# RWKV-7 attention and dropless experts on one core: paired products share PSUM banks, and the PE order weighs array time against instruction count

## The chip, the core and the metric

The kernel runs on 1 core of one Trainium2 chip. The metric is the device time of one execution in microseconds (us), the median of several; lower is better. Engines are named as the profile names them: PE (TensorE's matmuls) and PEld (its weight loads), DVE (VectorE), ACT (ScalarE), POOL (GpSimd), SP (SyncE, which here only issues DMAs).

## The reference

Two parts run one after the other. The first is a recurrence over 768 time steps for 4 x 8 heads of width 40:

```python
for t in range(S):
    y[:, :, t] = einsum('bhd,bhde->bhe', r_t, state)
    Sa = einsum('bhde,bhe->bhd', state, a_t)
    state = state * w_t[:, :, None, :] - einsum('bhd,bhe->bhde', Sa, b_t)
    state = state + einsum('bhd,bhe->bhde', v_t, k_t)
```

Its output, 3072 rows of 320 numbers, goes into a mixture of 8 experts: each row takes the expert with the largest of 8 logits, `relu(x @ w1[e]) @ w2[e]`, times the softmax weight of that expert.

## The kernel before

**Attention.** Time is cut into 12 chunks of 64 steps, and the batch into two halves, which gives 24 units of work (`unit(u)`, line 395; u = 2 * chunk + half). Each unit holds 16 heads as eight blocks of 64x64 in tiles of 128 partitions. Within a chunk the recurrence becomes products of 64x64 blocks. A unit loads its operands by SP (`load`, line 411, four DMAs for each of dec, KB twice, A, V2, R, Vu), takes running products of the decays by two scans on DVE (rv and q, lines 432 and 440), scales KB and A by them on POOL (lines 447 and 449), and then works on PE in these products, each into PSUM and from there to SBUF by ACT or DVE:

- `p_ka` (line 458) and the two of `p_n` (473): KB with A, masked by DVE into Gk, T and N
- `p_sq` (497): N,T and T,N, copied into the first X; then three times `p_power` and `p_sum` (508, 534), which square X and carry a sum along; the copies go to ACT or DVE, the half-sums (lines 488 and 491, three instructions) to DVE. The last round gives M and TT, and `p_last` (557) makes TF of them. This is the X chain, which inverts a triangular matrix
- transposes of V2 and KB (lines 573, 583), `p_rhs` (605, with the state ST), a transpose of ST to Sn, `p_uT` (631), `p_yr` (647: the state's rows, Sn with R), `p_z` (655: Vu with R, masked into ZU), transposes of Vu, `p_y` (679: nKB with ZU, into the banks that `p_yr` began), which gives the output and the new state, and `p_x` (705), which turns the output for storage and makes the logits.

A 64x64 product uses one quarter of the array; most products take the four quarters in rotation (`TILES`), `p_ka` two of them. One matmul of the program stands in the trace as two matmuls and two weight loads (a transpose as one of each).

**What sets the order.** A unit only records steps. `in_order` (line 212) then plays them through with a cost in us for each: it takes at every point the step that can start first, of equals the one with the lowest rank (`key`, line 262), gives it PSUM banks from the 8 there are (`Held(n)` asks for n banks, from the first step that uses them to the last), and emits it on its engine's queue. Steps marked ANY go to ACT or DVE. A PE step's n is its count of instructions; the player lets PE take 256 of them (`PAGE`) per 3.6 us (`FETCH`). Buffers come in rings (`Ring`); a ring of 2 (dec) lets unit u + 2 load when unit u has been read. Engines take their queues strictly in order.

**Routing and experts.** Behind the attention the kernel sorts rows by expert (DVE, POOL and PE), then gathers them, and runs two dense layers per expert on PE. The weights of expert 0 are fetched into a pool of their own: `first_weights` (751) is a step of rank 8, those of the others follow when the attention's memory is free. The change touches none of this code but the place of that fetch and of the constants that the routing uses.

Of the kernel before, what the change touches and what calls it, by code (L numbers as in the profile page):

```python
# [23 lines left out]
def kernel(  # L24
# [62 lines left out]
    before = consts.tile([128, 128], F32)  # L87
    nc.gpsimd.memset(before[:], 1.0)
    nc.gpsimd.affine_select(
        before[:], before[:], compare_op=ALU.is_gt, fill=0.0, base=0, pattern=[[1, 128]], channel_multiplier=-1,  # L90
    )

# [22 lines left out]

    ones_sq = consts.tile([128, 128], F32)
    nc.gpsimd.memset(ones_sq[:], 1.0)
    zero_e = consts.tile([128, E], F32)
    nc.gpsimd.memset(zero_e[:], 0.0)
    keep = consts.tile([128, E, NT], F32)  # L120
    nc.gpsimd.memset(keep[:], 1.0)
    nc.gpsimd.memset(keep[:, :, 0:1], 0.0)

    def counted(name, shape, pattern, base, mult=0):
        ti = consts.tile(shape, I32, name=name + "_i")
        tf = consts.tile(shape, F32, name=name)
        nc.gpsimd.iota(ti[:], pattern=pattern, base=base, channel_multiplier=mult)
        nc.gpsimd.tensor_copy(tf[:], ti[:])
        return tf
# [9 lines left out]
    iota_r = consts.tile([128, 128], F16)  # L139
    nc.gpsimd.tensor_copy(iota_r[:], iota_f[:])  # L140
# [3 lines left out]
    nc.gpsimd.tensor_scalar(tokc[HP:], tokc[HP:], scalar1=float(S - C), scalar2=None, op0=ALU.add)  # L144
    tokv = consts.tile([128, NT], F32)
    nc.gpsimd.tensor_copy(tokv[:, :NCH], tokc[:])
    nc.gpsimd.tensor_scalar(tokv[:, NCH:], tokc[:], scalar1=-1.0, scalar2=None, op0=ALU.mult)
# [3 lines left out]
    nc.gpsimd.memset(turn_gate[:, :, 128:], 0.0)  # L151
    for par in range(2):
        nc.scalar.dma_start(
            turn_gate[par * HP : par * HP + D, :, 128:], moe_w_gate.rearrange("(p a e) n -> a e p n", a=2, e=D)[par],
        )
    nc.gpsimd.tensor_scalar(turn_gate[:, :, 128:], turn_gate[:, :, 128:], scalar1=-1.0, scalar2=None, op0=ALU.mult)
    nc.gpsimd.tensor_copy(turn_gate[:, :, :128], ident[:, None, :].to_broadcast([128, NP, 128]))
# [25 lines left out]
    PAGE, FETCH = 256, 3.6  # L183
# [28 lines left out]
    def in_order():  # L212
# [3 lines left out]
        page = [0, 0.0]  # L216
# [26 lines left out]
        while ready:  # L243
            times = sorted({f for f in bank_free if f is not None})
            best = None
            for s, r in ready.items():
                new = [h for h in s.ps if h.at is None]
                for e in ((ACT, DVE) if s.eng == ANY else (s.eng,)):
# [13 lines left out]
                    key = (t0, s.rank, t0 + cost)  # L262
# [38 lines left out]
    with tc.tile_pool(name="ring", bufs=1) as ring, \  # L301
# [23 lines left out]
        r_dec = Ring("dec", [SEG * C1 + 1], 2)  # L325
# [34 lines left out]
        for i in range(3):  # L360
            for j, r in enumerate((r_KB, r_A, r_V2, r_Vu, r_R)):
                if i < len(r.bufs):
                    t, held = r.bufs[i]
                    for lo in (32, 96):
                        zero(-99 + 9 * i + j, POOL if lo == 32 else DVE, 0.5, t[lo : lo + 32], held)
        for t, held in r_qini.bufs:
            zero(-98, POOL, 0.6, t[:], held)
        for r in (r_rhs, r_ST, r_S):
            for t, held in r.bufs:
                zero(-50, POOL, 0.6, t[:], held)  # L370
# [4 lines left out]
        def pair(h, width):  # L375
            return psum[:, h.at : h.at + 2, : NP * width].rearrange("x a (p d) -> x a p d", p=NP)
# [18 lines left out]
        def unit(u):  # L395
# [28 lines left out]
            other = ACT if u == 0 else SP  # L424
# [14 lines left out]
            Step(pre, DVE, 0.3, invert, reads=hrv, writes=hqi + hpc)  # L439
# [17 lines left out]

            def p_ka(e, ps=ps):
# [4 lines left out]
            Step(u, PE, 8 * ROUND, p_ka, reads=hKB + hA, writes=[ps], n=64)  # L463
            Step(u, DVE, 0.69, lambda e, ps=ps: nc.vector.tensor_tensor(
                Gk[:], psum[:, ps.at, :].rearrange("x (q p j) -> x q p j", p=NP, q=2),
                m_plus[:, None, None, :].to_broadcast([128, 2, NP, C]), op=ALU.mult,
            ), reads=[ps], writes=hGk)
            T1, hT1 = r_T.take()
            N1, hN1 = r_N.take()
            for t1, ht1, mask, turned_ in ((T1, hT1, m_up, False), (N1, hN1, m_low, True)):  # L470
                ps = Held(2)

                def p_n(e, ps=ps, turned_=turned_):
                    t = pair(ps, C)
                    for p in range(NP):
                        for par, z in TILES:
                            q = par ^ z
                            l, r = b_at(p, q, par), head(Aq, p, q, par)
                            mm(t[halves[z], q, p, :], *((r, l) if turned_ else (l, r)))
                Step(u, PE, 4 * ROUND, p_n, reads=hKB + hA, writes=[ps], n=64)  # L480
                Step(u, DVE, 0.69, lambda e, ps=ps, t1=t1, mask=mask: nc.vector.tensor_tensor(  # L481
                    t1[:], pair(ps, C), mask[:, None, None, :].to_broadcast([128, 2, NP, C]), op=ALU.mult,
                ), reads=[ps], writes=ht1)
# [10 lines left out]
            for i, (l, r) in enumerate(((T1, N1), (N1, T1))):  # L494
                ps = Held(2)

                def p_sq(e, ps=ps, l=l, r=r):
                    t = pair(ps, C)
                    for p in range(NP):
                        for h, s in TILES:  # L500
                            q = h ^ s
                            mm(t[halves[s], q, p, :], l[halves[h], q, p, :], r[halves[h], q, p, :])
                Step(u, PE, 4 * ROUND, p_sq, reads=hN1 + hT1, writes=[ps], n=64)
                Step(u, ANY, 0.59, lambda e, i=i, ps=ps, X=X: copy(e, X[:, :, :, i, :], pair(ps, C)), reads=[ps], writes=hX[i : i + 1])
            Step(u, DVE, 1.1, lambda e, X=X: sums(e, X[:, :, :, 2, :], ihalf[:, None, None, :].to_broadcast([128, 2, NP, C]), T1[:], False),
                 reads=hT1, writes=hX[2:3])

            def p_power(e, ps, X, l, r):
                t = pair(ps, C)
# [4 lines left out]

            k = 2
            while 4 * k <= C:

                end = 4 * k == C
                Xn, hXn = r_X.take() if not end else (None, None)
                ps = Held(2)  # L520
                Step(u, PE, 4 * ROUND, lambda e, ps=ps, X=X: p_power(e, ps, X, 1, 0), reads=hX[:2], writes=[ps], n=64)
                if end:
                    M, hM = r_M.take()
                    Step(u, DVE, 0.69, lambda e, ps=ps, M=M: nc.vector.tensor_tensor(M[:], pair(ps, C), eye(2, NP), op=ALU.add),  # L524
                         reads=[ps], writes=hM)
                else:
                    Step(u, ANY, 0.59, lambda e, ps=ps, Xn=Xn: copy(e, Xn[:, :, :, 0, :], pair(ps, C)), reads=[ps], writes=hXn[0:1])
                ps = Held(2)
                w = 1 if end else 2

                def half_sums(ps, w):
                    return psum[:, ps.at : ps.at + 2, : NP * w * C].rearrange("x b (p w j) -> x b p w j", p=NP, w=w)

                def p_sum(e, ps=ps, X=X, w=w):
# [487 lines left out]
```

## Time and profile before

| | before |
|---|---|
| median of 3 runs | 901.5 us (900.42 to 902.14) |
| the profiled execution: its own time | 899.75 us |
| its span in the trace, first to last instruction | 898.0 us |
| mean granted clock of TensorE | 0.955 |
| PE busy | 776.2 us (86%), 17128 matmuls |
| PEld busy | 606.5 us (68%), 17128 weight loads |
| DVE busy | 460.0 us (51%) |
| ACT busy | 234.5 us (26%) |
| POOL busy | 173.7 us (19%) |

Busy times are sums over the whole span; the stages have different limits, so a share of the span says little of any one of them. The granted clock is in shares of the full 2.4 GHz; it has two levels, 1.00 and 0.50.

### The profile page before, as it was taken

To read this page: it belongs to the slowest core of one execution; us is meant where nothing else is said; L and a number is where in the kernel's file an instruction comes from. 1 tells how busy PE (TensorE), PEld (TensorE's weight loads), DVE (VectorE), ACT (ScalarE), POOL (GpSimd) and SP (SyncE) were. 2 spreads that over 40 slices of the span, in tenths; PEclk is the share of its full clock that TensorE was granted. 3 is DMA by queue.
4 is the path that set the end of the run, shared out by engine and by line. 5 is a ranking of instruction groups with operands and counts; after the bars stand their busy time and mean duration, and the time that the engine had idled before them with its cause. 6 is when DMAs were issued, how large, how long until landed. Compare 5 with 4: busy or idle time off the path is not lost.

```text
span 898.0 us, 38059 instructions
## 1 busy us (share of the span) xinstructions
PE 776.2 (86%) x17128; PEld 606.5 (68%) x17128; DVE 460.0 (51%) x980; ACT 234.5 (26%) x502; POOL 173.7 (19%) x224
## 2 busy tenths in 40 slices
PE   0797789889998999899989998418999999999995
PEld 0686678788887888788878887416845545545543
DVE  6685578777676867687767676361110110120110
ACT  0343244333333334333433433100110110110110
POOL 9332111121202020202020100043211211001001
PEclk9999899999999989999999999656999999999998
DMA  5323313222322232223222200183313513402000
GB/s 165 89 67 86 86 45 69 65 65 60 71 67 61 57 71 64 56 61 75 62 57 60 48 12 12 22 259 96 95 53 107 187 60 114 132 14 83 10 13 23
DMA packets 136569, 65.16 MB, mean 73 GB/s; under 512 B 116881, under 2 KB 132243, under 8 KB 136404
## 3 DMA queue, kind: packets, MB, share of 16 engines
q1 hardware_dynamic: 130888, 52.76, 23.2%
q0 software_dynamic: 3136, 9.44, 3.4%
q8 instruction: 135, 2.21, 1.0%
q10 hardware_dynamic: 2380, 0.50, 0.3%
q14 instruction: 30, 0.25, 0.1%
HBM read 54.01 MB, written 9.31 MB: 71 GB/s over the span
## 4 chain that ended last, share of the span: by engine, by line
issue 36%; PE 30%; DVE 11%; DMA 9%; POOL 7%; SPq 3%; ACT 2%; POOLq 0%; ACTq 0%; DVEq 0%
PE ps L385 25%; DMA dec<-in_packed_dram 8%; PE ps L583 4%; DVE X L491 3%; POOL out_dram L917 3%; SPq L416 3%; POOL xg L875 2%; PE ps L573 2%; ACT X L380 2%; DVE X L488 1%; DVE q L440 1%; DVE T L481 1%; POOL KB L447 1%; DMA KB<-in_packed_dram 1%; DVE TT L491 0%
## 5 line engine op out<-in xcount | busy, mean ns | idle before, releaser
L385 PE MATMUL ps<-X 64*64 64x64 f32 (+1 forms) x6144 | 163.1, 243 | 22.2 <-DVE X L491 10.9
L385 PEld LDWEIGHTS ps<-X 64*64 64x64 f32 x6144 | 133.8, 135 | 42.2 <-DVE X L491 15.4
L901 DVE TENSOR_SCALAR h_sb<-hp 128x448 f32<-128x448 f32 (+2 forms) x44 | 21.8, 497 | 227.1 <-PE hp L900 225.8
L910 PE MATMUL zp<-w,h_sb 128*128 128x320 f32 (+1 forms) x512 | 123.8, 433 | 0.0
L380 ACT COPY X<-ps 128x512 f32<-128x512 f32 x152 | 88.3, 586 | 125.6 <-PE ps L385 119.9
L894 PE MATMUL hp<-xgT,w 128*128 128x448 f32 (+2 forms) x352 | 115.0, 473 | 3.7 <-DVE h_sb L901 2.3
L910 PEld LDWEIGHTS zp<-w,h_sb 128*128 128x128 f32 (+1 forms) x512 | 80.6, 177 | 37.5 <-issue 2.4
L894 PEld LDWEIGHTS hp<-xgT,w 128*128 128x128 f32 x352 | 60.9, 208 | 53.1 <-issue 48.9
L447 POOL TENSOR_TENSOR KB<-KB,rv 128x512 f32<-128x512 f32 x48 | 59.0, 1249 | 133.9 <-DMA A<-in_packed_dram 48.6
L449 POOL TENSOR_TENSOR A<-A,q 128x512 f32<-128x512 f32 x24 | 29.2, 1215 | 248.9 <-PE ps L385 83.8
L917 POOL DMA_INDIRECT out_dram<-zo,s_idx x28 | 27.6, 987 | 185.1 <-ACT zo L916 183.8
L491 DVE TENSOR_TENSOR X<-ps,X 64x256 f32<-64x256 f32 x144 | 60.8, 422 | 3.1
L902 ACT ACTIVATE h_sb<-hp 128x448 f32<-128x448 f32 (+2 forms) x44 | 19.3, 442 | 159.9 <-PE hp L900 121.6
L488 DVE TENSOR_TENSOR X<-ps,X 128x256 f32<-128x256 f32 x72 | 30.4, 422 | 46.4 <-ACT X L380 45.8
L385 PE MATMUL ps<-R,Vu 64*128 64x64 f32 x768 | 51.0, 284 | 2.5 <-issue 1.2
L385 PE MATMUL ps<-A,KB 64*64 64x64 f32 x1536 | 45.3, 224 | 9.0 <-DVE M L524 8.4
L385 PEld LDWEIGHTS ps<-R,Vu 64*128 64x128 f32 x768 | 47.4, 196 | 5.0 <-issue 2.4
L385 PEld LDWEIGHTS ps<-A,KB 64*64 64x64 f32 x1536 | 40.6, 138 | 12.0 <-DVE M L524 8.6
L432 DVE TENSOR_TENSOR_SCAN rv<-dec,ones 128x521 f32<-128x521 f32 x24 | 29.7, 1239 | 34.7 <-DMA dec<-in_packed_dram 22.8
L663 DVE TENSOR_TENSOR ZU<-ps,m_plus 128x512 f32<-128x512 f32 x48 | 30.9, 685 | 28.8 <-PE ps L385 28.6
L916 ACT COPY zo<-zp 128x320 f32<-128x320 f32 x28 | 11.9, 425 | 119.8 <-PE zp L910 115.9
L385 PE MATMUL ps<-ZU,nKB 128*64 128x104 f32 (+1 forms) x768 | 39.6, 257 | 1.0 <-DVE ZU L663 0.8
(178 smaller groups left out, 1066.1 us busy)
## 6 DMA issues: line engine op xcount, KB each, us to landing
w<-in_moe_w_dram SPq DMA_DIRECT2D x8, 1280.0 KB
w<-in_moe_w_dram SPq DMA_DIRECT2D x8, 1024.0 KB
KB<-in_packed_dram SPq DMA_DIRECT2D x188, 40.0 KB
x_rows<-xs SPq DMA_DIRECT2D x48, 96.0 KB
dec<-in_packed_dram SPq DMA_DIRECT2D x96, 40.0 KB
V<-in_packed_dram SPq DMA_DIRECT2D x96, 40.0 KB
Vu<-in_packed_dram SPq DMA_DIRECT2D x96, 40.0 KB
A<-in_packed_dram SPq DMA_DIRECT2D x92, 40.0 KB
```

Of the source, the lines that this page charges most:

```text
L380: nc.scalar.copy(dst, src)
L385: nc.tensor.matmul(out_, lhsT=lhsT, rhs=rhs, start=start, stop=stop, skip_group_check=True)
L432: Step(pre, DVE, 1.4, lambda e: nc.vector.tensor_tensor_scan(rv[:, : SEG * C1 + 1][:, ::-1], dec[:, ::-1], ones65[:, ::-1], 0.0, op0=ALU.m ...
L447: Step(pre, POOL, 1.25, lambda e, kb=kb, by=by: nc.gpsimd.tensor_tensor(kb, kb, by, op=ALU.mult), reads=hrv, writes=hKB[i : i + 1])
L449: Step(pre, POOL, 1.22, lambda e: nc.gpsimd.tensor_tensor(Aq[:], Aq[:], q3[:, :, :C], op=ALU.mult), reads=hq, writes=hA)
L488: nc.vector.tensor_tensor(dst[:, 0], src[:, 0], old[:, 0], op=ALU.add)
L491: nc.vector.tensor_tensor(dst[o_, 1], src[o_ if o else halves[h], 1], old[halves[h], 1], op=ALU.add)
L583: nc.tensor.transpose(psum[:, ps.at + b // NP, b % NP * 128 : (b % NP + 1) * 128], at(*divmod(b, 2)).rearrange("x s t -> x (s t)"), ident[:],)
L663: Step(u, DVE, 0.69, lambda e, s=s, ps=ps: nc.vector.tensor_tensor(ZU[:, s, :, :C], psum[:, ps.at + s, :].rearrange("x (b j) -> x b j", j= ...
L894: nc.tensor.matmul(hp[:, : c1 - c0], lhsT=w[0][:, db, (fb + i) * 128 : (fb + i + 1) * 128], rhs=xT[:, db, c0:c1], start=(db == 0), stop=False,
L910: nc.tensor.matmul(zp[r0 : r0 + n], lhsT=h[:, fb, c0 : c0 + n], rhs=w[2][:, fb, :], start=(fb == 0), stop=(fb == FB - 1), skip_group_check ...
L917: ins_ = nc.gpsimd.indirect_dma_start(out=out[:, :], out_offset=bass.IndirectOffsetOnAxis(ap=si, axis=0), in_=zo[:], in_offset=None, bound ...
```

## The change

- Products that came in pairs, each with two PSUM banks of its own, now share two banks: the two of `p_n`, the two of `p_sq`, and the last power and sum (`p_end`). In `p_n` the two take turns matmul by matmul, on the same quarter; in the others one follows the other. What reads them starts after the pair.
- `p_yr` is no step any more: its matmuls are the first of `p_y`, so that `p_y`'s two banks are held from there.
- The planner's key: among steps that can start at the same time, a PE step's rank is raised by the distance from even between the array time handed out so far (its costs) and 0.0134 us per instruction. Costs are set anew.
- dec has a ring of 3 instead of 2. Loads of unit 1 that SP had go to ACT's queue, as those of unit 0 did.
- The routing's constants are written on POOL by a step of rank 12, turn_gate is loaded by POOL instead of ACT, and the memsets stand in another order.
- The weights of expert 0 are fetched after half of the units.

```diff
-    PAGE, FETCH = 256, 3.6
+    PAGE, FETCH, FIRST = 256, 3.6, 190
+    PACE = 0.0134
...
-        page = [0, 0.0]
+        page = [FIRST, FETCH]
+        even = 0.0
...
                     cost = s.cost * (1.17 if s.eng == ANY and e == DVE else 1.0)
-                    key = (t0, s.rank, t0 + cost)
+
+                    uneven = 2 * abs(even + s.cost - s.n * PACE) if s.n else 0.0
+                    key = (t0, s.rank[0] + uneven, s.rank, t0 + cost)
...
+            if s.n:
+                even = min(1.0, max(-1.0, even + s.cost - s.n * PACE))
...
-        r_dec = Ring("dec", [SEG * C1 + 1], 2)
+        r_dec = Ring("dec", [SEG * C1 + 1], 3)
...
+        Step(-80, POOL, 1.5, fill_turn_gate, writes=[h_tg], lag=3)
+        Step(-1, POOL, 0.2, turn_sign, writes=[h_tg])
+        Step(12, POOL, 8, route_constants)
...
-            other = ACT if u == 0 else SP
+            other = ACT if u < 2 else SP
...
-            for t1, ht1, mask, turned_ in ((T1, hT1, m_up, False), (N1, hN1, m_low, True)):
-                ps = Held(2)
-
-                def p_n(e, ps=ps, turned_=turned_):
-                    t = pair(ps, C)
...
-                            mm(t[halves[z], q, p, :], *((r, l) if turned_ else (l, r)))
-                Step(u, PE, 4 * ROUND, p_n, reads=hKB + hA, writes=[ps], n=64)
...
+            ps = Held(2)
+
+            def p_n(e, ps=ps):
+                for p in range(NP):
+                    for par, z in TILES:
+                        q = par ^ z
+                        l, r = b_at(p, q, par), head(Aq, p, q, par)
+                        mm(pair(ps, C, 0)[halves[z], q, p, :], l, r)
+                        mm(pair(ps, C, 1)[halves[z], q, p, :], r, l)
+            Step(u, PE, 8 * ROUND, p_n, reads=hKB + hA, writes=[ps], n=128)
...
-            for i, (l, r) in enumerate(((T1, N1), (N1, T1))):
-                ps = Held(2)
...
-                Step(u, PE, 4 * ROUND, p_sq, reads=hN1 + hT1, writes=[ps], n=64)
...
+            ps = Held(2)
+
+            def p_sq(e, ps=ps):
+                for w, (l, r) in enumerate(((T1, N1), (N1, T1))):
...
+            Step(u, PE, 8 * ROUND, p_sq, reads=hN1 + hT1, writes=[ps], n=128)
...
+            def p_end(e, ps=ps, X=X):
+                p_sum(e, pair(ps, C, 1).unsqueeze(3), X, 1)
+                p_power(e, pair(ps, C, 0), X, 1, 0)
+            Step(u, PE, 8 * ROUND, p_end, reads=hX, writes=[ps], n=128)
...
-            before_z = []
-            if c:
-                def p_yr(e):
-                    for p in range(NP):
-                        for q, par in TILES:
-                            mm(y_at()[halves[par], q, p, :C], Sn[halves[q], p, par, :], R_[halves[q], p, par, :], start=(p == 0), stop=False)
-                before_z = [Step(u, PE, 4 * ROUND, p_yr, reads=hSn + hR, writes=[psy], n=64)]
...
             def p_y(e):
+                if c:
+                    for p in range(NP):
+                        for q, par in TILES:
+                            mm(y_at()[halves[par], q, p, :C], Sn[halves[q], p, par, :], R_[halves[q], p, par, :], start=(p == 0), stop=False)
...
+            if u == NU // 2:
+                half_way = steps[-1]
...
-        Step(8, SP, 2.0, first_weights)
+        Step(8, SP, 2.0, first_weights, after=[half_way])
```

On PE, in the middle of the attention, the planner before laid six products of 64 instructions each in a row (x16 is 16 matmuls of the program; names are the tiles that a product reads, numbers the buffers; 64x64 is the output of one matmul):

```order
L385 MATMUL ps<-TT_197,M_195 64x64 x16
L385 MATMUL ps<-N_189,T_187 64x64 x16
L385 MATMUL ps<-T_187,N_189 64x64 x16
L385 MATMUL ps<-TF_199,rhs_201 64x64 x16
L385 MATMUL ps<-nV_179,Gk_184 64x40 x16
L385 MATMUL ps<-ST_204,A_152 64x40 x16
L385 MATMUL ps<-R_154,Vu_162 128x64 x16
L583 MATMUL ps<-ident,Vu_162 128x128 x8
```

The same products of a pair of units in the order now:

```order
L406 MATMUL ps<-N_159,T_157 64x64 x16
L406 MATMUL ps<-T_157,N_159 64x64 x16
L603 MATMUL ps<-ident,KB_129 128x128 x8
L406 MATMUL ps<-R_123,S_176 64x64 x16
L406 MATMUL ps<-ZU_178,nKB_150 64x104 x16
L406 MATMUL ps<-X_163 64x64 x32
L406 MATMUL ps<-X_164 64x128 x16
L406 MATMUL ps<-X_164 64x64 x16
L406 MATMUL ps<-A_122,KB_130 64x64 x16
L406 MATMUL ps<-TT_167,M_165 64x64 x16
L406 MATMUL ps<-turn_gate,xT_184 128x136 x4
L406 MATMUL ps<-TF_169,rhs_171 64x64 x16
```

Transposes, `p_y` (ZU,nKB, now with R,S directly ahead of it) and `p_x` (turn_gate) stand between the products of 64 instructions.

On SP's queue, from the kernel's start. Before:

```order
L170 DMA w_226<-in_moe_w_dram 128x2x1024
L172 DMA w1c<-in_moe_w_dram 64x4x128 x2
L175 DMA w_228<-in_moe_w_dram 128x8x320
L416 DMA dec_165<-in_packed_dram 40x4x64 x4
L416 DMA dec_166<-in_packed_dram 40x4x64 x4
L416 DMA V_157<-in_packed_dram 40x4x64 x4
```

Now:

```order
L437 DMA dec_134<-in_packed_dram 40x4x64 x4
L437 DMA dec_135<-in_packed_dram 40x4x64 x4
L437 DMA V_126<-in_packed_dram 40x4x64 x4
L437 DMA KB_128<-in_packed_dram 40x4x64 x4
L437 DMA Vu_131<-in_packed_dram 40x4x64 x4
L437 DMA V_127<-in_packed_dram 40x4x64 x4
L437 DMA KB_129<-in_packed_dram 40x4x64 x4
L437 DMA Vu_132<-in_packed_dram 40x4x64 x4
L437 DMA dec_136<-in_packed_dram 40x4x64 x4
```

The fetch of the weights is gone from the head of the queue, and the third dec load no longer waits for the first dec buffer to be read.

## Rows read from the trace of the kernel before

**Rows 1.** Windows: busy us (x instructions) per engine, then PEclk, DMA share, GB/s.
```profile
core 0: us, PE busy (x) PEld busy (x) DVE busy (x) ACT busy (x) POOL busy (x), PEclk, DMA share, GB/s
27.60:577.00 549.40, 489.94 (x15965) 437.20 (x15964) 390.37 (x821) 200.04 (x424) 89.59 (x92) 0.97 0.26 60
```
**Rows 2.** DMA queues in 27.6 to 577 us: packets, MB, share of 16 engines.
```profile
q8 instruction: 125, 2.05, 1.5%
```
**Rows 3.** Windows, 493 to 508 us.
```profile
493.00:508.00 15.00, 13.63 (x563) 12.17 (x552) 10.65 (x24) 6.70 (x15) 3.74 (x4) 1.00 0.22 51
```
**Rows 4.** Timeline of PE, 502 to 508 us: start, us, operation, count, [idle before <-releaser].
```profile
503.59 0.65 PE L385 MATMUL ps<-T,N 64*64 64x64 f32 x32
504.06 0.65 PE L385 MATMUL ps<-TF,rhs 64*64 64x64 f32 x32
...
505.74 0.30 PE L385 MATMUL ps<-ST,A 64*64 64x40 f32 x8
506.66 0.56 PE L385 MATMUL ps<-ST,A 64*64 64x40 f32 x24 [0.62 <-issue]
```
**Rows 5.** Timeline of PE, 303 to 310 us.
```profile
303.48 2.00 PE L385 MATMUL ps<-R,Vu 64*128 64x64 f32 x32
305.41 1.09 PE L583 MATMUL ps<-ident,Vu 128*128 128x128 f32 x8
306.43 1.58 PE L385 MATMUL ps<-X 64*64 64x64 f32 x64
307.94 1.65 PE L385 MATMUL ps<-ZU,nKB 128*64 128x104 f32 x32
309.52 1.09 PE L583 MATMUL ps<-ident,KB 128*128 128x128 f32 x8
```
**Rows 6.** Waits of PE, 27 to 577 us: total us, times, longest.
```profile
PE ps L385 <- issue: 12.5, 18, 1.2
PE ps L385 <- DVE X L491: 10.9, 25, 0.6
...
PE ps L385 <- ACT X L380: 3.8, 7, 0.8
PE ps L385 <- DVE ZU L663: 2.9, 3, 1.8
PE ps L385 <- DVE X L488: 2.6, 9, 0.6
```
**Rows 7.** Page, costliest groups: busy us, mean ns of one | idle before, releaser.
```profile
L491 DVE TENSOR_TENSOR X<-ps,X 64x256 f32<-64x256 f32 x144 | 60.8, 422 | 3.1
L488 DVE TENSOR_TENSOR X<-ps,X 128x256 f32<-128x256 f32 x72 | 30.4, 422 | 46.4 <-ACT X L380 45.8
```
**Rows 8.** Timeline of PE at 340 us, a product of `p_ka` and the next.
```profile
339.86 1.15 PE L385 MATMUL ps<-A,KB 64*64 64x64 f32 x32
340.94 0.66 PE L573 MATMUL ps<-ident,V 128*128 128x128 f32 x4
```
**Rows 9.** Timeline of all engines, 80 to 93 us (SPq: the time of issuing).
```profile
82.89 5.83 SPq L416 DMA_DIRECT2D dec<-in_packed_dram  x4
...
90.30 1.24 DVE L432 TENSOR_TENSOR_SCAN rv<-dec,ones 128x521 f32<-128x521 f32 x1 [8.40 <-DMA dec<-in_packed_dram]
...
92.18 1.13 PE L385 MATMUL ps<-A,KB 64*64 64x64 f32 x31 [8.45 <-DVE M L524]
```
**Rows 10.** Windows, 87 to 97 us.
```profile
87.00:97.00 10.00, 4.82 (x124) 4.30 (x128) 6.37 (x12) 1.17 (x2) 2.33 (x2) 0.50 0.37 86
```
**Rows 11.** Timeline of POOL and PE, 0 to 30 us.
```profile
3.84 0.20 POOL L117 MEMSET ones_sq<- 128x128 f32 x1
...
7.80 0.94 POOL L350 MEMSET KB<- 32x1024 f32 x1
...
23.93 2.52 POOL L447 TENSOR_TENSOR KB<-KB,rv 128x512 f32<-128x512 f32 x2 [1.08 <-DMA KB<-in_packed_dram]
...
27.63 2.24 PE L385 MATMUL ps<-A,KB 64*64 64x64 f32 x63
```
**Rows 12.** Waits of DVE, 22 to 577 us: total us, times, longest.
```profile
DVE X L488 <- ACT X L380: 45.8, 55, 2.4
```

More of the change, by code (lines that the diff above doesn't have):

```diff
@@ L151, with route_constants @@
[L151 to L157, printed above, removed]
+    def route_constants(e):
+        nc.gpsimd.memset(before[:], 1.0)
+        nc.gpsimd.affine_select(
+            before[:], before[:], compare_op=ALU.is_gt, fill=0.0, base=0, pattern=[[1, 128]], channel_multiplier=-1,
+        )
+        nc.gpsimd.memset(ones_sq[:], 1.0)
+        nc.gpsimd.memset(zero_e[:], 0.0)
+        nc.gpsimd.memset(keep[:], 1.0)
+        nc.gpsimd.memset(keep[:, :, 0:1], 0.0)
+        for ti, tf, pattern, base, mult in iotas:
+            nc.gpsimd.iota(ti[:], pattern=pattern, base=base, channel_multiplier=mult)
+            nc.gpsimd.tensor_copy(tf[:], ti[:])
+        nc.gpsimd.tensor_copy(iota_r[:], iota_f[:])
+        nc.gpsimd.tensor_scalar(tokc[HP:], tokc[HP:], scalar1=float(S - C), scalar2=None, op0=ALU.add)
+        nc.gpsimd.tensor_copy(tokv[:, :NCH], tokc[:])
+        nc.gpsimd.tensor_scalar(tokv[:, NCH:], tokc[:], scalar1=-1.0, scalar2=None, op0=ALU.mult)
@@ L360 @@
         for i in range(3):
[L361 removed]
+            for j, r in enumerate((r_KB, r_A, r_V2, r_R, r_Vu)):
                 if i < len(r.bufs):
@@ L456, in unit, with masked @@
             ps = Held(1)
+            def masked(u, by, t, held, ps, src, mask):
+                if by == DVE:
+                    Step(u, DVE, 0.69, lambda e: nc.vector.tensor_tensor(t, src(), mask, op=ALU.mult), reads=[ps], writes=held)
+                else:
+                    Step(u, ACT, 0.59, lambda e: nc.scalar.copy(t, src()), reads=[ps], writes=held)
+                    Step(u, POOL, 1.2, lambda e: nc.gpsimd.tensor_tensor(t, t, mask, op=ALU.mult), writes=held)
             def p_ka(e, ps=ps):
@@ L462, in p_ka @@
                             mm(psum[halves[par], ps.at, (q * NP + p) * C : (q * NP + p + 1) * C], KB[halves[par], p, q, par, :], head(Aq, p, q, par))
[L463 to L467, printed above, removed]
+            Step(u, PE, 1.0, p_ka, reads=hKB + hA, writes=[ps], n=64)
@@ new lines, in unit @@
+                Step(u, DVE, 1.29, lambda e, ps=ps, X=X, Xn=Xn: sums(
+                    e, Xn[:, :, :, 2, :], half_sums(ps, 2)[:, :, :, 1, :], X[:, :, :, 2, :], True,
+                ), reads=[ps] + hX[2:3], writes=hXn[2:3])
+                X, hX = Xn, hXn
+                k *= 2
+            M, hM = r_M.take()
+            TT, hTT = r_TT.take()
+            ps = Held(2)
+            def p_end(e, ps=ps, X=X):
+                p_sum(e, pair(ps, C, 1).unsqueeze(3), X, 1)
+                p_power(e, pair(ps, C, 0), X, 1, 0)
@@ L554, in unit @@
+            Step(u, PE, 8 * ROUND, p_end, reads=hX, writes=[ps], n=128)
+            Step(u, DVE, 1.29, lambda e, ps=ps, X=X, TT=TT: sums(e, TT[:], pair(ps, C, 1), X[:, :, :, 2, :], True), reads=[ps] + hX[2:3], writes=hTT)
+            Step(u, DVE, 0.69, lambda e, ps=ps, M=M: nc.vector.tensor_tensor(M[:], pair(ps, C, 0), eye(2, NP), op=ALU.add), reads=[ps], writes=hM)
             TF, hTF = r_TF.take()
@@ L660, in p_z @@
                                Vu[halves[q], p, 2 * par : 2 * par + 2, :].rearrange("x s t -> x (s t)"), R_[halves[q], p, par, :])
-            Step(u, PE, 1.71, p_z, reads=hV + huT + hR, writes=[ps], after=before_z, n=64)
+            Step(u, PE, 1.93, p_z, reads=hV + huT + hR, writes=[ps], n=64)
             for s in range(2):
```

131 lines of the change are left out of this document (53 added, 78 removed).

## The prediction

> **What bounds the kernel now.** I read the stretches first. From PE's first product of KB and A to its last of the attention, 27.6 to 577 us, it is 549.4 us [rows 1]; the 321 us behind that (routing and experts, to the span's 898.0) the change leaves alone. So the question is the 549.4 us. There PE is busy for 489.9 us and VectorE (DVE) for 390.4 us, and PE's records are 15,965 matmuls and 15,964 weight loads, 31,929 instructions [rows 1]. The reader is to see that a busy PE is here not the whole story: the instructions themselves have to arrive. The instruction queue q8 brought 125 packets in that stretch [rows 2], so a packet holds about 31,929 / 125 = 255 instructions (256, as the planner's constant PAGE has it). Where PE runs nothing but small products, they set the pace: in 493 to 508 us it ran 563 + 552 = 1,115 instructions in 15 us [rows 3], 13.5 ns each or 3.45 us per packet. A product on quarters of the array, 64 instructions, takes 0.47 us when it runs free (T,N, from its start at 503.59 to that of the next product at 504.06), 7.3 ns each, twice the pace of arrival. Two products on, ST,A stops after 8 of its 32 matmuls, and the other 24 follow 0.9 us later, with idle time that ends on no semaphore ("issue") [rows 4].
>
> The Trainium skill (Runtime: NRT & Kernel Launch, Instruction fetch mechanics) says that crossing from one such block to the next is mostly hidden; by it the mixing term below would be 0. The rows show otherwise here.
>
> Against that stand the products that occupy the array long with few instructions: R,Vu 1.93 us for 64, the eight transposes of Vu 1.02 us for 16, ZU,nKB 1.58 us for 64, and a little less so X (a power and its double-width sum), 1.5 us for 128, each from its start to that of the next [rows 5]. Summed over all products of the attention these durations give 441 us of array time; the 31,952 instructions at 13.5 ns give 431 us. The two limits are equal, so what counts is their mix within each packet. I went through the order of before in blocks of 256 instructions and gave each block the larger of its array time and 3.45 us: 483 us. To that come PE's waits for other engines, of which the largest stand in [rows 6] (the whole list without "issue" is 44 us), and 3% of clock, 16 us, for a mean of 0.97 [rows 1]. 483 + 44 + 16 = 543 of 549 us. The account closes, so I forecast by its terms.
>
> **The change part by part.** *Mixing (the planner's key).* The same blocks in the new order, with the same durations, give 466.5 us: the shortfall below 3.45 us falls from 44.5 to 28.1 us, the spread of a block's array time from 0.97 to 0.62 us. Only part of the unevenness goes: 61 of 125 blocks are still short, against 57. Term: **-16 us**; 0 if arrival isn't the limit, -25 if the blocks lend to each other across a border.
>
> *Shared banks and the sum in p_y (short holds).* The number of matmuls stays. What they buy is room for other work between two links of the X chain, whose next product waits for copies and half-sums. PE's waits for X are 10.9, 3.8 and 2.6 us, 17.3 us in all [rows 6]. I counted in both orders how much array time lies between the last product of one X and the first that reads the next, for the 72 links: 24 have at most 1.12 us in between before, 3 after; the half-sums alone are three instructions of 0.42 us, 1.27 us [rows 7]. I keep a quarter of the waits: **-13 us**, between 0 (the waits turn up elsewhere) and -17. Adding the state rows within p_y moves 64 instructions past p_z and the Vu transposes and costs nothing: they ran anyway. A merged product frees its first result up to 0.47 us later, at three places per unit; the median room between links is still 2 us, which hides it. Without that cover it would be 3 x 0.47 x 24 = 34 us, which is more than the term gains.
>
> *p_n takes its two products in turns on the same quarter.* No row of before shows that. The nearest are N,T, four quarters in rotation, whose twin T,N takes 0.47 us for 32 recorded matmuls [rows 4], and A,KB of p_ka, two quarters, 1.08 us for 32 [rows 8]. Every matmul of the order (x16) is already two records on one quarter (x32), and T,N still gets four quarters' pace. So I take **0**; the far end is a rival below.
>
> *Third dec buffer.* At 82.89 us SP issues the four dec loads over 5.83 us; the scan of rv, at the head of DVE's queue, starts at 90.30 after 8.40 us of waiting for them, and PE, which waits for M behind it, goes on at 92.18 after 8.45 us [rows 9]. The granted clock is 0.50 from 87 to 97 us [rows 10], the lower level (1.2 GHz), in and behind that hole, which costs 10 x 0.5 = 5 us more. With a third buffer the load stands a unit earlier on SP's queue. Term **-13.5 us**, bounds 0 and -13.5. What is late next is ZU, 2.9 us [rows 6].
>
> *Start.* POOL writes the routing's constants from 3.84 us on, and its first memset of KB starts at 7.80; the first KB product follows at 23.93, PE at 27.63 [rows 11]. Now the constants stand behind the A product of unit 1, which brings POOL forward by about 5 us; two DMA issues of turn_gate move onto POOL, which take up to 1 us each if they are like its indirect ones. SP no longer issues 2.6 MB of weights ahead of dec. Term **-3 us**, bounds 0 and -8. The constants, those 5 us, now stand ahead of the KB product of unit 2; what hides them are units 0 and 1, at 549.4 / 24 = 22.9 us of PE each.
>
> *Weights in the middle.* Loads behind them on SP's queue share the DMA engines with 2.6 MB; cover are the rings of three units, some 40 us. Term 0, up to +8 without that cover.
>
> Sum: -16 - 13 - 13.5 - 3 = **-45.5 us**. The profiled execution took 899.75 us, 1.75 us below the median of 901.5. So 899.75 - 45.5 + 1.75 = **856 us** on the median's scale.
>
> **The rivals.** *The waits move.* DVE is busy 390.4 us of the stage and waits 45.8 us for ACT's copies before its half-sums [rows 12]; 436 us fill 79% of the stage now and 87% of a stage of 504 us. In an in-order queue as full as that, X's waits would come back as waits for ZU, TT or T. Then the -13 us go: 869 us. For it: DVE's work is the same, and the sums stay on DVE. Against it: the counted room between links.
>
> *Arrival isn't the limit* and the 13.5 ns are what the waits leave over: the -16 us go, 872 us. Against it: the stop inside ST,A.
>
> *Slower: the quarter is taken in order.* If a matmul may not start before the one ahead of it in the program, the 64 records of p_n run on one quarter at a time. At 0.47 us for 32 in four quarters, one quarter alone needs 4 x 0.47 = 1.9 us for 32 and 3.8 us for 64, instead of 0.94: +2.8 us per unit, 24 x 2.8 = +67 us; where one quarter's last record overlaps the next one's first, three quarters of that time, 2.8 us, +45 us. Result 901 to 923 us, about 912. It decides from 2.8 us per p_n on (45.5 / 24 = 1.9 above 0.94). Against it: T,N's pace with two records per matmul. The Trainium skill (TensorE: Matmul & The Clock Gate, Part 3, What overlaps and what doesn't) states that matmuls start in strict program order; that would give this rival, and it doesn't fit with T,N's 0.47 us.
>
> That the change doesn't do what it says is out for the order, which the printed rows show; its effect on the blocks is partial, and counted so.
>
> **How the numbers follow.** Forecast (with terms within their bounds, 840 to 866) 0.57; the waits move 0.18, arrival isn't the limit 0.10 (both with some of the other's loss, 866 to 885); more than forecast, because the remaining waits and low clock shrink as well (below 840) 0.07; slower by the quarter 0.06; nothing left of the gain for reasons not named 0.02. The range leaves out the quarter, the lower half of the best case and the upper end of the two middle ones: **830 to 882 us**. A measurement of this kernel tells 0.2% (1.8 us) from no change. Faster 0.92, same 0.02, slower 0.06.
>
> **What would show it.** In the profile after: the attention stage ends at 528 to 535 us instead of 577, PE's instruction count unchanged; q8's packets of the stage stay at 125, at some 4.0 us apiece instead of 4.4; PE's waits for X add up to about 5 us; no hole of several us at 80 to 95 us and no low clock there; first A,KB products at 24 to 25 us; p_n's 64 matmuls in about 1 us. Wrong I am if p_n takes over 2 us, if DVE's waits for PE shrink while PE's for DVE stay near 40 us, or if the stage ends early but the experts' start doesn't move with it.

## The result, and the profile after

The changed kernel takes **864.0 us** (median of 4, 861.1 to 871.7) against 901.8 for the one before in the same session: ratio 0.959 [0.952, 0.966], some 37 us faster; a second measurement beside the last experiments gave 0.960 [0.954, 0.967]. The forecast was 856 in 830 to 882. The sum held; the parts it was made of, as the experiments show, mostly did not, so that the hit is in good part luck. The ratio is known to 0.7% each way, where the prediction counted on 0.2%. The profiled execution took 866.43 us, with a span of 864.7.

In the profile after, the attention stage (first product of KB and A to the last turn_gate) is 515.6 us long, against 549.4 [rows 1]; it ends at 541.8 us, where 528 to 535 were forecast. Windows of it, with the columns of [rows 1]:

```profile
26.20:541.80 515.60, 479.46 (x15961) 436.73 (x15960) 392.09 (x827) 194.60 (x416) 94.10 (x118) 0.96 0.29 67
62.00:72.00 10.00, 8.57 (x148) 8.01 (x152) 3.96 (x10) 1.93 (x4) 2.32 (x2) 0.50 0.33 75
80.00:95.00 15.00, 14.40 (x458) 12.80 (x460) 11.22 (x26) 5.96 (x14) 1.42 (x2) 1.00 0.26 61
```

The instructions are as many as before, so are the packets that bring them (DMA queues of the stage), which now come every 515.6 / 125 = 4.1 us:

```profile
q8 instruction: 125, 2.05, 1.7%
```

The hole at 80 to 95 us is gone: PE is busy for 14.4 of 15 us at full clock there. But 62 to 72 us now runs at the lower level. PE's waits in the stage (total us, times, longest), to be held against [rows 6]:

```profile
PE ps L406 <- issue: 7.6, 11, 2.8
PE ps L406 <- DVE X L516: 5.4, 8, 2.3
PE ps L406 <- DVE N L482: 4.6, 3, 4.1
PE ps L406 <- DVE Gk L482: 3.4, 1, 3.4
PE ps L406 <- DVE M L573: 3.3, 4, 2.0
PE ps L406 <- DVE X L513: 2.9, 2, 2.6
PE ps L406 <- DVE ZU L676: 2.3, 3, 1.2
```

L516 and L513 are the half-sums that were L491 and L488. X's waits are 5.4 + 2.9 = 8.3 us where they were 17.3 [rows 6]; new are single long ones for N and Gk. M's waits, which held the hole of 8.4 us before, are down to 3.3 us from

```profile
PE ps L385 <- DVE M L524: 9.5, 3, 8.4
```

The long waits lead to those of DVE, in the profile after:

```profile
DVE X L513 <- ACT X L401: 35.6, 33, 2.9
DVE rv L453 <- DMA dec<-in_packed_dram: 26.9, 9, 5.9
```

The first is smaller than in [rows 12] (45.8). The second was 19.5 us, 8 times, before. With a third buffer DVE waits *longer* for dec. Timeline of all engines, two of these places:

```profile
25.32 4.15 SPq L437 DMA_DIRECT2D dec<-in_packed_dram  x4
...
26.21 0.51 PE L406 MATMUL ps<-A,KB 64*64 64x64 f32 x8
...
30.98 1.24 DVE L453 TENSOR_TENSOR_SCAN rv<-dec,ones 128x521 f32<-128x521 f32 x1 [3.97 <-DMA dec<-in_packed_dram]
...
32.72 0.68 DVE L482 TENSOR_TENSOR Gk<-ps,m_plus 128x512 f32<-128x512 f32 x1
...
33.46 0.68 PE L406 MATMUL ps<-nV,Gk 64*64 64x40 f32 x32 [3.43 <-DVE Gk L482]
...
51.22 6.81 SPq L437 DMA_DIRECT2D dec<-in_packed_dram  x4
...
59.64 1.24 DVE L453 TENSOR_TENSOR_SCAN rv<-dec,ones 128x521 f32<-128x521 f32 x1 [2.44 <-DMA dec<-in_packed_dram]
...
62.69 0.68 DVE L482 TENSOR_TENSOR N<-ps,m_low 128x512 f32<-128x512 f32 x1
...
63.42 1.14 PE L406 MATMUL ps<-N,T 64*64 64x64 f32 x32 [4.08 <-DVE N L482]
```

The scan of a unit that PE will need much later stands at the head of DVE's in-order queue; the masks that PE needs now stand behind it. The Trainium skill (PSUM — Partial Sum Buffer, Engine vs sequencer instructions) calls the queues of ScalarE, VectorE and GpSimd strict FIFO; for DVE these rows agree.

The product whose price the prediction left to a rival, `p_n` with its two results in turns on one quarter (timeline of PE):

```profile
101.42 0.36 PE L406 MATMUL ps<-A,KB 64*64 64x64 f32 x8
101.58 0.32 PE L406 MATMUL ps<-KB,A 64*64 64x64 f32 x8
...
102.40 0.27 PE L406 MATMUL ps<-X 64*64 64x128 f32 x1
102.45 0.22 PE L406 MATMUL ps<-KB,A 64*64 64x64 f32 x2
...
102.50 0.22 PE L406 MATMUL ps<-KB,A 64*64 64x64 f32 x1
```

1.0 us for all of it, and its records do not start in the order of the program: there the two products alternate matmul by matmul, here eight records of one start before the first of the other, and the first record of the next product (X) starts at 102.40, ahead of the last of `p_n` at 102.50. So what was said ahead, that engines take their queues strictly in order, is not what PE's starts show here against the program as it is written; whether the compiler had changed the order is not on record.

To compare all runs I sorted, in each stage, the gaps over 0.2 us between the starts of successive PE instructions (each less 0.05 us) by whether the later one waits on a semaphore (in the table "semaphore gaps"; "stops without" are the others, and "lower clock" is the time at the granted clock of 0.50). "Blocks" is the sum over the 256-instruction blocks of the planned order, as in the prediction; ratios are to the kernel before, which took 906 to 908 us in the sessions of the experiments. Ratios compare within a session; the columns from the stage on are single traces, and those of the first two rows come from the first session. The change traced a second time (a0) has a stage 8.6 us longer, so a stage difference of that size between two rows shows nothing by itself.

| kernel | ratio [95%] | stage us | semaphore gaps | stops without | lower clock | blocks |
|---|---|---|---|---|---|---|
| before | 1 | 548.7 | 80.6 | 23.2 | 28.5 | 482.8 |
| changed | 0.959 [0.952, 0.966] | 515.2 | 48.6 | 17.9 | 39.2 | 466.5 |
| a0_change_again | 0.960 [0.954, 0.967] | 523.8 | some 54 | some 20 | 40.5 | 466.5 |
| a1_unmixed | 0.987 [0.979, 0.994] | 545.5 | 59.5 | 40.0 | 44.3 | 476.2 |
| a3_long_holds | 1.028 [1.020, 1.036] | 573.7 | 107.5 | 9.2 | 44.7 | 461.2 |
| b1_mixed | 1.041 [1.035, 1.048] | 591.1 | 121.2 | 5.7 | 65.2 | 460.0 |
| b3_short_holds | 0.974 [0.968, 0.981] | 526.1 | 44.0 | 36.3 | 23.9 | 488.1 |
| e1_six_banks | 1.000 [0.996, 1.003] | 559.1 | 87.7 | 15.9 | 52.0 | 463.4 |
| a2_two_dec | 0.965 [0.960, 0.971] | 517.1 | 48.1 | 22.4 | 24.4 | 465.5 |
| b4_dec_planned_late | 0.976 [0.971, 0.982] | 539.8 | 69.0 | 24.3 | 21.8 | 482.0 |
| c1_dec_planned_late | 0.936 [0.930, 0.941] | 499.2 | 28.8 | 29.2 | 6.8 | 462.5 |
| c3_weights_end | **0.928** [0.922, 0.934] | 493.8 | 28.1 | 24.4 | 0 | 462.5 |
| c5_end_two_dec | 0.937 [0.932, 0.943] | 503.4 | 31.7 | 27.0 | 12.0 | 461.9 |
| d1_more_instructions | 0.947 [0.939, 0.955] | 515.1 | 29.8 | 31.4 | 6.8 | 481 |

What is left of a stage without both kinds of gap is 441 us in c3, which never falls to the lower clock: the array time of the prediction. In the kernel before it is 444.9, in b1, with most of the lower clock, 464.2.

### The profile page after: what moved, and what is told of

Same layout as the page of the kernel before. It is cut to its first block, busy times and chain, and to the rows that moved or that the text cites. A ratio compares the mean times of both kernels' runs of the same rounds, so it can differ in the third digit from the quotient of the medians.

```text
span 864.7 us, 38029 instructions
## 1 busy us (share of the span) xinstructions
PE 767.2 (89%) x17128; PEld 607.9 (70%) x17128; DVE 464.2 (54%) x991; ACT 229.7 (27%) x495; POOL 178.5 (21%) x226
## 4 chain that ended last, share of the span: by engine, by line
issue 36%; PE 32%; DVE 11%; POOL 8%; DMA 8%; SPq 3%; ACT 1%; POOLq 0%; DVEq 0%; ACTq 0%
PE ps L406 27%; DMA dec<-in_packed_dram 6%; POOL out_dram L936 3%; SPq L437 3%; PE ps L603 3%; POOL xg L894 3%; DVE X L516 2%; PE ps L593 2%; DVE X L513 1%; DVE q L461 1%; DVE rv L453 1%; DVE TT L516 1%; DVE M L573 1%; DVE ZU L676 1%; ACT X L401 1%
## 5 line engine op out<-in xcount | busy, mean ns | idle before, releaser
L406 PE MATMUL ps<-X 64*64 64x64 f32 (+1 forms) x6144 | 153.5, 243 | 10.2 <-issue 3.8
L406 PEld LDWEIGHTS ps<-X 64*64 64x64 f32 x6144 | 131.1, 136 | 22.5 <-issue 8.4
L920 DVE TENSOR_SCALAR h_sb<-hp 128x448 f32<-128x448 f32 (+2 forms) x44 | 21.8, 498 | 228.4 <-PE hp L919 221.7
L401 ACT COPY X<-ps 128x512 f32<-128x512 f32 x166 | 95.7, 587 | 157.0 <-PE ps L406 136.3
L929 PEld LDWEIGHTS zp<-w,h_sb 128*128 128x128 f32 (+1 forms) x512 | 80.6, 177 | 37.4 <-issue 2.4
L468 POOL TENSOR_TENSOR KB<-KB,rv 128x512 f32<-128x512 f32 x48 | 59.6, 1263 | 135.2 <-DMA KB<-in_packed_dram 65.2
L470 POOL TENSOR_TENSOR A<-A,q 128x512 f32<-128x512 f32 x24 | 28.5, 1187 | 180.7 <-DVE g L742 59.3
L516 DVE TENSOR_TENSOR X<-ps,X 64x256 f32<-64x256 f32 x144 | 60.8, 422 | 3.2
L406 PE MATMUL ps<-A,KB 64*64 64x64 f32 x1536 | 57.7, 229 | 4.3 <-DVE X L516 2.7
L406 PEld LDWEIGHTS ps<-A,KB 64*64 64x64 f32 x1536 | 53.1, 137 | 7.3 <-DVE X L516 3.1
L406 PEld LDWEIGHTS ps<-R,Vu 64*128 64x128 f32 x768 | 48.1, 199 | 3.9 <-ACT Vu L661 0.9
L513 DVE TENSOR_TENSOR X<-ps,X 128x256 f32<-128x256 f32 x72 | 30.1, 419 | 35.9 <-ACT X L401 35.6
L453 DVE TENSOR_TENSOR_SCAN rv<-dec,ones 128x521 f32<-128x521 f32 x24 | 30.5, 1270 | 32.0 <-DMA dec<-in_packed_dram 26.9
L894 POOL DMA_INDIRECT xg<-x_rows,g_idx x28 | 26.8, 958 | 54.3 <-PE tp L902 44.5
```

The lines of the kernel that those rows point to most:

```text
L401: nc.scalar.copy(dst, src)
L406: nc.tensor.matmul(out_, lhsT=lhsT, rhs=rhs, start=start, stop=stop, skip_group_check=True)
L453: Step(pre, DVE, 1.4, lambda e: nc.vector.tensor_tensor_scan(rv[:, : SEG * C1 + 1][:, ::-1], dec[:, ::-1], ones65[:, ::-1], 0.0, op0=ALU.m ...
L468: Step(pre, POOL, 1.25, lambda e, kb=kb, by=by: nc.gpsimd.tensor_tensor(kb, kb, by, op=ALU.mult), reads=hrv, writes=hKB[i : i + 1])
L470: Step(pre, POOL, 1.22, lambda e: nc.gpsimd.tensor_tensor(Aq[:], Aq[:], q3[:, :, :C], op=ALU.mult), reads=hq, writes=hA)
L513: nc.vector.tensor_tensor(dst[:, 0], src[:, 0], old[:, 0], op=ALU.add)
```

## The experiments

**Mixing taken out of the change (a1_unmixed).**

```diff
-uneven = 2 * abs(even + s.cost - s.n * PACE) if s.n else 0.0
+uneven = 0 * abs(even + s.cost - s.n * PACE) if s.n else 0.0
```

> The changed kernel (864.0 us) with the planner's unevenness weight set from 2 to 0, everything else kept: the order goes back to plain ranks, the short holds, the third dec buffer and the corrected costs stay. The blocks of 256 instructions, each at the larger of its array time and 3.45 us, sum to 476.2 us, against 466.5 with the weight. Theory (instruction arrival bounds a block): +10 us, 874, and the stretches with small products alone stop at the borders of blocks again. Rival 'Arrival isn't the limit': no change beyond 3 us, 861 to 867. Second rival, waits for dec and X reshuffled by any new order: up to 8 us either way, with the sum of PE's waits in the trace changing by that much.

Measured 0.987: against the change's 0.960, 0.027 x 902 = 24 us slower, more than twice the 10 us that the blocks gave. The stops without a semaphore go from 17.9 us (some 20 in a0) to 40.0 (the profile's "issue" from 7.6 to 25.0): 20 to 22 us, most of the 24. That these stops are waits for instructions, the traces show directly. In all fourteen there are 239 stops of over 0.5 us without a semaphore (8 in the change, 30 in a1). Counted over PE's and PEld's records, each falls at the same place of a block of 256 instructions, and each ends 1.2 to 1.7 us after the end of a packet on q8. Of the gaps on semaphores, 1 of 28 in a1 falls at that place. So arrival is a limit and the mixing removes its stops, against the rival.

**Mixing alone (b1_mixed).** In the kernel before the new key, with the new costs of PE's steps:

```diff
-key = (t0, s.rank, t0 + cost)
+uneven = 2 * abs(even + s.cost - s.n * PACE) if s.n else 0.0
+key = (t0, s.rank[0] + uneven, s.rank, t0 + cost)
...
-Step(u, PE, 8 * 2 * w / 2400, p_y, reads=hnKB + (hZU[:2] if last else hZU), writes=[psy], n=64)
+Step(u, PE, 16 * 0.95 * w / 1000, p_y, reads=hnKB + (hZU[:2] if last else hZU), writes=[psy], n=64)
```

> The kernel before (901.8 us) with the planner's mixing alone: the unevenness in its key and the corrected array times of PE's steps (R,Vu 1.93, nKB,ZU 1.58, transposes 0.59 and 1.02); holds, dec buffers, start and weights as before. The blocks sum to 460.0 us against 482.8. Theory: -23 us from arrival, 879, if the waits stay at their 44 us; X waits may grow by some us since the holds are long. Rival 'Arrival isn't the limit': within 5 us of 902.

Neither theory: 37 us *slower*, though the stops fall from 23.2 to 5.7 us as expected. The waits on semaphores rise by 41 us, and time at the lower clock more than doubles. PE's waits there:

```profile
PE ps L390 <- DVE X L493: 14.9, 11, 6.2
PE ps L390 <- DVE X L496: 14.6, 38, 0.6
PE ps L390 <- DVE ZU L668: 9.6, 9, 3.1
PE ps L390 <- ACT X L385: 8.9, 21, 0.8
PE ps L390 <- issue: 2.4, 5, 0.7
```

They are the X chain's and ZU's, which [rows 6] has (L488 and L491 there) at 2.6, 10.9, 2.9 and 3.8 us.

**Short holds taken out of the change (a3_long_holds).** `p_n`, `p_sq`, the last power and sum and `p_yr` as in the kernel before, for instance:

```diff
-Step(u, PE, 8 * ROUND, p_n, reads=hKB + hA, writes=[ps], n=128)
+    Step(u, PE, 4 * ROUND, p_n, reads=hKB + hA, writes=[ps], n=64)
```

> The changed kernel with the old hold structure: T and N, the two squares, the last power and its sum are steps with two banks each again, and the state rows are a product of their own ahead of R,Vu; the planner's mixing, the costs and the third dec buffer stay. The blocks sum to 461.2 us (466.5 in the changed kernel), so by arrival alone it would be 5 us faster, 859. The prediction's short-hold term says +13 us of X waits: 864 - 5 + 13 = 872. Rival 'The waits move' (short holds bring nothing): 859 to 864.

Measured 1.028, 61 us slower than the change: nearly five times the term of 13. Semaphore gaps 107.5 us against 48.6, stops 9.2.

**Short holds alone (b3_short_holds).** The same edit, forward, in the kernel before (with the changed kernel's costs of the half-sums and of `p_y`).

> The kernel before (901.8 us) with the short holds alone: T and N, the two squares, and the last power with its sum share two banks each, and the state rows are added within the y product; planner's key, costs, dec buffers, start and weights as before. The blocks sum to 488.1 us against 482.8. The prediction's term -13 for X waits, +5 for the blocks: 894. The theory after the first runs (the two parts act on one another: the mixing puts PE's products of a chain behind others, which only short holds leave room for) also expects a small effect here, 885 to 900, though with the mixing the same edit is worth 58 us (changed kernel against the one with long holds). Rival (short holds are worth their 58 us by themselves): 845 to 855.

0.974, 23 us faster (879), a little more than the 885 to 900 expected and far from the rival's 850. Semaphore gaps 80.6 to 44.0; stops 23.2 to 36.3, up by a third of what was won: packets that arrived during waits now come too late.

**Why holds matter (e1_six_banks).** All short holds and the mixing stay; the planner has six banks.

```diff
-bank_free = [0.0] * 8
+bank_free = [0.0] * 6
```

(and the search for free banks runs over six).

> The changed kernel with the planner allowed six of the eight PSUM banks, nothing else: the short holds, the mixing and the costs stay, and the blocks sum to 463.4 us (466.5). Theory (what the short holds give back is PSUM banks, of which the mixed order needs more): PE's waits on semaphores, 48.6 us in the changed kernel's stage, go up to 90 to 120 us, as in the run with long holds (107.5): 1.00 to 1.04 of the kernel before. Rival (the prediction's reason, room between the links of the X chain, which the merged products give by themselves): under 10 us slower, 0.96 to 0.97.

1.000: the whole gain is gone. Semaphore gaps 87.7 us, just short of the range expected. So the merged products do not bring the gain by themselves, as room between the links, which was the prediction's reason; it hangs on the number of free banks. The plan's own account (its costs, no measurement) points the same way: PE's steps are put off for want of banks by 34 us in the kernel before, 47 in b1, 54 in a3, 23 here, under 5 in the change and in b3.

Banks are not all of it, though. DVE's waits for dec, 26.9 us in the change and 19.5 before, are longer as well in e1, a3 and b1, in this order:

```profile
DVE rv L453 <- DMA dec<-in_packed_dram: 42.6, 15, 6.1
DVE rv L453 <- DMA dec<-in_packed_dram: 44.0, 15, 6.1
DVE rv L437 <- DMA dec<-in_packed_dram: 45.3, 18, 8.5
```

Of PE's semaphore gaps, those that touch such a wait or the 2 us behind it make 26, 31 and 31 us there, 16 in the change and 12 in the kernel before: 10 of the 39 us that e1 adds to the change's gaps, 15 of the 59 of a3, 19 of the 41 that b1 adds to those of the kernel before. No run has few banks or long holds together with a dec load that is planned truly, so how much is left for the banks alone stays open.

**Two dec buffers in the change (a2_two_dec).**

```diff
-r_dec = Ring("dec", [SEG * C1 + 1], 3)
+r_dec = Ring("dec", [SEG * C1 + 1], 2)
```

> The changed kernel with two dec buffers again, nothing else. The blocks sum to 465.5 us (466.5). The prediction's term says +13.5 us: 877. The theory now (VectorE's wait for dec comes from a scan that the plan puts at the head of its queue before the load has landed, whatever the number of buffers): within 6 us of the changed kernel either way, 858 to 870, and VectorE's wait for dec again between 18 and 35 us.

0.965 against 0.960, 5 us with intervals that overlap; DVE's wait for dec is 21.6 us (26.9 with three). The 13.5 us are not there.

**dec's load described truly, in the change (c1_dec_planned_late) and in the kernel before (b4_dec_planned_late).** The same edit in both; cost and lag are 4.2 and, from the third unit on, 8 for dec, and stay 1.7 and 2.5 for all else:

```diff
-Step(u - 3, eng, 1.7, fn, writes=held, lag=2.5)
+Step(u - 3, eng, cost, fn, writes=held, lag=lag)
```

> The changed kernel with one load described truly to the planner: dec's four transfers cost SP 4.2 us instead of 1.7 and land 8 us later instead of 2.5 (from the third unit on), so the scan of rv is not put at the head of VectorE's queue before its data are there. Nothing else differs, though the planner's order shifts: the blocks sum to 462.5 us (466.5). In the changed kernel VectorE waits 26.9 us for dec, and three PE gaps behind that (3.70, 4.29 and 2.89 us) with 14 us at the lower clock follow. Theory (a scan planned too early in an in-order queue, not the number of buffers, makes the stall): VectorE's wait for dec under 8 us, no such gap, 4 us from the blocks, 10 us from the gaps and some 5 us of clock: 845 to 854. Rival (the load itself is late, whatever the plan says): the wait turns into one of POOL or PE for KB and A, 860 to 866.

> The kernel before with the dec load described truly to the planner (4.2 us of SP, landing 8 us later), two buffers kept, nothing else. The blocks sum to 482.0 us (482.8). Theory (the plan makes the stall): VectorE's wait for dec falls from 19.5 to under 6 us, the 8.45 us hole at 83.5 to 92.2 us and the low clock behind it go: 883 to 890. Rival (two buffers are too few, as the prediction had it): the wait stays or moves to POOL's products of KB and A, 897 to 903.

0.936 and 0.976: 22 us off the change and 21 us off the kernel before, with two buffers there. In both DVE's wait for dec is gone from the list altogether, and 80 to 95 us of b4 reads 13.92 us busy at full clock, against 6.55 before. The trace of b4 has a stage only 8.9 us shorter than that of the kernel before, which is from the faster first session; the 21 us are from runs of one session. The plan let the scan follow 4.2 us after the first issue; the rows above need 5.7 to 8.4 us (25.32 to 30.98, 51.22 to 59.64): SP waits 44 times, 71.9 us in all, for an earlier transfer into the same dec before it issues the next. Both gains are a little beyond the ranges expected.

**Weights at the end (c3_weights_end).** In c1 the weights still move in the middle. Timeline of PE there, the three stops, and below it the DMA queues of 322 to 337 us in c1:

```profile
325.21 0.99 PE L406 MATMUL ps<-X 64*64 64x128 f32 x27 [1.08 <-issue]
...
332.24 0.26 PE L406 MATMUL ps<-nV,Gk 64*64 64x40 f32 x3 [3.30 <-issue]
...
336.53 0.49 PE L406 MATMUL ps<-X 64*64 64x64 f32 x6 [0.75 <-issue]
```

```profile
q1 hardware_dynamic: 4033, 3.02, 70.5%
q8 instruction: 3, 0.05, 1.3%
```

```diff
-if u == NU // 2:
+if u == NU - 1:
```

> The first run with dec planned late (0.9355 of the kernel before), with the first expert's weights issued behind the attention's last store instead of in the middle; PE's order is the same. In that run PE stops for 1.35, 3.52 and 1.06 us at 324 to 336 us with no semaphore, the instruction queue's packets start 6.8 us apart instead of some 4, and 6.8 us at the lower clock follow, just where the 2.6 MB of weights move. Theory (the weights' transfer holds up the instruction packets): these three stops and the low clock go, -6 to -9 us, and at the end the experts start as before since DMA is nearly idle during the routing, +0 to +3: 0.927 to 0.933 of the kernel before. Rival (the stops are there anyway, the weights don't matter): 0.935 to 0.937, with stops of the same length at the same place. Second rival (the weights come too late for the experts): over 0.940, PE waits for w behind the routing.

0.928 against 0.936 in another session (the intervals overlap). The stage is 5.4 us shorter, which two traces of one kernel can differ by; the place tells more. With the same order of PE, the stops between 318 and 337 us shrink from 6.3 to 2.3 us, the longest distance of two packet starts between 30 and 515 us falls from 6.85 (just there) to 5.21 us, and the lower clock is gone:

```profile
322.00:337.00 15.00, 13.04 (x464) 11.58 (x463) 11.80 (x28) 6.83 (x16) 3.74 (x4) 1.00 0.29 68
```

(c1 has 9.87 us of PE there, at 0.88 and a DMA share of 0.72.) The change's own longest stop without a semaphore, 2.77 us up to 345.96, also lies behind the weights, which SP issues there from 332.6 us on. The experts do not wait for the late weights: from the stage's end to the span's it is 319.5 us, 322.9 in the change. This is the fastest version found, some 65 us below the kernel before.

**Two buffers in that version (c5_end_two_dec).** The same edit in c3.

> The run with the weights at the end (0.928 of the kernel before), with two dec buffers instead of three. Theory (the plan's landing time, not the buffer, decides): within 4 us of it, 0.924 to 0.933, VectorE's wait for dec under 8 us. Rival (the prediction's term, the third buffer is worth 13.5 us): 0.940 to 0.945.

0.937: between the two, with an interval that overlaps that of c3. DVE never waits for dec, so not by that wait; of the 8 us, 1.7 are a later first product (26.6 against 24.9), the rest small waits, stops and 12 us of lower clock of a shifted order. That the buffer itself is worth it stays open.

**The price of an instruction (d1_more_instructions).** In c3, ahead of each TF,rhs product:

```diff
+mm(t[halves[q], z ^ q, p, 0:1], rhs[halves[z], q, p, :], TF[halves[z], q, p, 0:1])
```

> The run with the weights at the end (0.928 of the kernel before) with 16 products of one column added ahead of TF,rhs in each of the 24 units, into the place that TF,rhs then overwrites: 64 more PE instructions per unit, 1,536 in all, planned order unchanged. Theory (arrival at 13.5 ns per instruction bounds the blocks): the blocks sum to 481 us against 462.5, so +17 to +21 us, 0.947 to 0.952, six more packets on the instruction queue, PE's time without a semaphore grows and its other waits shrink a little. Rival 'Arrival isn't the limit': only their array time, 0 us to at most 24 x 0.47 = 11 us, if a product of one column takes as long as one of 64: 0.928 to 0.940.

0.947: 0.019 x 902 = 17 us slower (5 to 29 by the ends of the two intervals), six more packets, in the trace 21.3 us more of stage for 1,536 instructions, 13.9 ns each. This is the size of the arrival price, but the run does not separate it from the rival's upper end of 11 us. By the table the stops grow by 7.0 us only, the other waits do not shrink (28.1 to 29.8), and 12.6 us lie in what is left of the stage without both (441.3 to 453.9), because a one-column product turned out to take as long as a full one:

```profile
219.31 1.16 PE L406 MATMUL ps<-TF,rhs 64*64 64x1 f32 x64
220.40 0.66 PE L593 MATMUL ps<-ident,ST 128*128 128x128 f32 x4
```

1.09 us for both together, twice 0.47 and a little.

**The change once more (a0_change_again).**

> The changed kernel once more, unaltered, so that the runs beside it have it on their own chip: 0.953 to 0.966 of the kernel before, as measured at first (0.959).

0.960, as at first.

## Why the prediction was right, and where it was not

The time was right; of its four terms none had the size given, and their errors cancelled, which is luck. The account of the kernel before closed in the same way: it had 483 - 441 = 42 us for arrival and 44 us of waits, where the gaps of the trace are 23.2 us of stops and 80.6 us on semaphores. By the first trace of the change, of 33.5 us that the stage lost, 32 are waits on semaphores and 5.3 stops without one; 11 us more at the lower clock took some 5 back.

- **Mixing, -16.** The mechanism was right: stops without a semaphore shrink (a1, b1), and the Trainium skill's "mostly hidden" (Runtime: NRT & Kernel Launch, Instruction fetch mechanics) does not hold here, with 40.0 us of stops in a1. The step that failed is adding it as a term of its own. Alone it costs 37 us; on top of the short holds it is worth 24. Even blocks need steps of different units open at once; that these want banks is what e1 and the plan's account point to, and in b1 nearly half of the added waits lie at dec's scan instead.
- **Shared banks and the sum in p_y, -13.** 23 us alone, 61 with the mixing. X's waits fell to 8.3 us, near the 5 forecast, but the reason given ("room for other work between two links") was the wrong one: the same merged products with six banks give nothing (e1). A wait of PE for the half-sums can also be one for the bank they read, which the traces do not tell apart; and a part of what a3 loses lies at dec's scan.
- **Third dec buffer, -13.5.** Failed, with the sentence "the load stands a unit earlier on SP's queue". It doesn't: the load still leaves just ahead of KB's, and the plan puts the scan where it believes the data land. The hole at 83 us went and three others came (3.43 and 4.08 us above, 2.62 us up to 108.73). DVE's wait rose from 19.5 to 26.9 us. What the term was after is real, about 21 us, but it lies in the planned landing time (b4, c1).
- **Start, -3.** KB's product on POOL starts at 21.00 us instead of 23.93 [rows 11], PE's at 26.21 instead of 27.63, where 24 to 25 were forecast: 1.4 us. POOL came forward by 2.9 us, not 5; by [rows 11] the constants take 7.80 - 3.84 = 4.0 us. The next 3.43 us stop, behind the scan of the third unit, gave it back.
- **Weights in the middle, 0 (up to +8).** Some 5 to 7 us, near the upper bound; but not by the loads behind them, as the bound assumed: the weights' packets delay those of the instructions.
- **p_n in turns, 0.** Right, 1.0 us. With it falls the slower rival. The Trainium skill (TensorE: Matmul & The Clock Gate, Part 3, What overlaps and what doesn't) has matmuls start and end in strict program order; against the program as written, the starts at 102.40 and 102.50 above do not agree. The 2.8 us more per `p_n` were the prediction's own price for such an order and not the page's: that one matmul starts after another does not mean that it waits for its end, so T,N's 0.47 us did not speak against the page.
- **The rivals.** "Arrival isn't the limit" fell with a1. "The waits move" was right in part: some moved to N and Gk, through dec's scan, but did not eat the gain. Slower by a quarter in order did not come; a slower kernel was to be had by another way that was not listed, the mixing without the banks.

## What to carry to other kernels

Waits for other engines and waits for instructions hide one another: whoever removes the first exposes late packets (b3), and whoever orders for even arrival needs more steps and their buffers open at once (b1), so two such edits are priced together, not summed. In a kernel whose order a planner fixes, a stall on an in-order queue is first a question of what landing time the plan believes; compare that with the trace before adding a buffer. Here the bulk transfer cost least where PE was idle anyway (c3).

## What was not expected of the hardware

A product with one column per matmul took PE as long as one with 64 (d1: 1.09 us for both, 16 matmuls of the program and 64 instructions each, on four quarters): the columns made no difference to its time. Each of PE's stops of over 0.5 us without a semaphore stood at the same place of a block of 256 instructions and ended 1.2 to 1.7 us behind the end of a packet (under a1). And 2.6 MB of weights on the data queue held the instruction queue's packets up to 6.85 us apart where the median is 3.8, which stopped PE for 3.3 us; 6.8 us at the lower clock went with it and were gone in c3.
